# First transposes in four PSUM tiles, ones under the keys by fills, two sets of squares at other places, dense work rounded to the piece

## The chip, the cores and the metric

The kernel runs on one core of a Trainium2 chip. The metric is the device time in microseconds (us) of one execution; lower is better. The core has a matrix engine (TensorE; PE in the profile, PEld for its weight loads), VectorE (DVE), ScalarE (ACT), GpSimd (POOL) and SyncE (SP), which here only issues DMAs.

## The reference

The input `x` has 2048 rows of 512. It is normalised per row. From that come sliding-window attention with 32 heads of 16 and a window of 256 keys, and a gated feed-forward layer with 1792 hidden columns:

```python
xn = _layernorm(x)
# attention A: q, k, v = xn @ wqkv, per head
scores = q @ k.T * Dh ** -0.5          # key within 0..255 rows behind the query
s = (softmax(masked scores) @ v) @ wo
# feed-forward B
g = _silu((_silu(xn @ w1) * (xn @ w3)) @ w2)
return x + s * g
```

Input and output are float32.

## The kernel before

**Precision.** Each float32 operand of a dense product is split into two float16 halves, `hi` and `lo`, after scaling by a power of two. A dense product is three matmuls, hi x hi, hi x lo, lo x hi. To find the power of two of a weight, `squares` (L175 on ScalarE, L177 on VectorE) sums the squares of each row into `ssq`, a cast makes `sb` (L187), and `powers` (L200) sums `sb` over the partitions with a matmul against `onesb`; L202 to L211 turn that into the scale. The float16 halves are then made by `split` (L215 `hi` on ScalarE, L216 `lo` on VectorE) or by `split_pool` (L224, L225 on ScalarE, L221 on GpSimd).

**Tiles.** The rows are cut into four tiles of 512 (t = 0 to 3). `prepare(t)` loads four blocks of 128 rows, centres and scales them (L337), transposes each by four matmuls against the identity (L353) and makes `XH` (L356) and `XL` (L361). For t = 0 the transposes of two blocks write the two halves of one PSUM tile of the pool `pss`.

**Attention.** A group g is 8 heads. `project` makes q and k of a group (L421, evacuated by L430 and L434, stored to DRAM by L437 to L441), and `fetch` (L453) loads them back with three float16 terms of each head under one another, 48 rows, in partitions 0 to 47 and 64 to 111 of `KA[r]` (r = 0, 1, 2 in rotation) and of `qa`. Rows 48, 49, 112 and 113 of `KA` hold the constant 2^12 ("ones"), against which the same rows of `qa` carry the negative row maximum. A unit is (t, g, p), p being one half of a group's heads; there are 32. `pass1` makes scores (L474) and row maxima (L479) of the unit two ahead, `pass2` makes scores again (L521), adds masks (L530 over 1024 columns, L535 over 512), takes the exponential (L539) and multiplies by V (L549).

**Feed-forward.** The 1792 hidden columns are 14 blocks f. `load(0, f)` loads block f's float32 weights; `measure(f, 1)` squares those of blocks f and f + 1, finds their scales and makes float16 halves; `gate_up` multiplies (L682; L693 tanh, L697 product, L702, L706, L221 behind it), `down` accumulates (L727).

**Order.** On TensorE the instructions run in the order in which the kernel writes them. On the other engines the order was chosen when the program was built; `tc.issue_after(i)` puts what its block writes behind instruction i on i's engine. `later(n, f)` calls f at the n-th next `step()`; `step()` comes after each batch and each dense piece. `spread` puts the dense pieces of a unit (6 matmuls each, some 9 or 3) between its seven batches of scores; a batch is up to one `pass2` chunk and one or two `pass1` parts, and batches 2, 4 and 6 also run the products with V, counted as 6. `keep_busy(n)` runs n matmuls that nothing reads. PSUM has three buffers of the pool `psm` (tag "mm"), two of `pss` (two banks each) and one of `pso`.

The start, for orientation (before the change):

```python
keep_busy(22)
...
run([k00[0], q00[0], k00[1], q00[1]])
qk[1][2]()
qk[1][3]()
with tc.issue_after(lasts["hi"].ins):
    run([k00[2], q00[2]])
```

`qk[g]` are load, squares, scale and split of the q and k weights of group g; `wv` the same of the v weights.

Of the kernel before, what the change touches and what calls it, by code (L numbers as in the profile page):

```python
# [1 line left out]

# [6 lines left out]
F32 = mybir.dt.float32  # L9
BF16 = mybir.dt.bfloat16  # L10
F16 = mybir.dt.float16
I32 = mybir.dt.int32
AF = mybir.ActivationFunctionType
ALU = mybir.AluOpType
# [5 lines left out]
P = 128  # L20
# [9 lines left out]
TW = S // NT  # L30
KW = TW + 2 * P
WIN = 64 + 2 * P
FB = F // P
# [9 lines left out]
TERMS = 3  # L43
KR = TERMS * DH
ONE = 2.0**12
VW = DH + 1
VB = 10
SLOTS = 32
# [13 lines left out]
def tile_block(ctx: ExitStack, tc: tile.TileContext, x, wqkv, wo, w1, w3, w2, out):  # L62
    nc = tc.nc
# [18 lines left out]
    pss = pool("pss", 2, PSUM)  # L82
    pso = pool("pso", 1, PSUM)
# [5 lines left out]
    def take(dtype):  # L89
        slot = free.pop(0)  # L90
        made = fpool.tile([P, 512 if dtype == F32 else 1024], dtype, name=slot, tag=slot, bufs=1)
        held[id(made)] = slot, made
        return made

    def give(*tiles):
        for made in tiles:
            free.append(held.pop(id(made))[0])
# [14 lines left out]
    def later(n, f):  # L112
        made_so_far[0] += 1
        queue.append((now[0] + n, made_so_far[0], f))
# [93 lines left out]

    def scaled(a, by, name):
        t = const.tile([P, 1], F32, name=name)  # L210
        nc.vector.tensor_scalar(t, a, by, None, op0=ALU.mult)  # L211
        return t

    def split(hi, lo, raw, s):
# [91 lines left out]
    def prepare(t):  # L306

        mv = lnpool.tile([P, 4, 2], F32, name="mv")
        rs = lnpool.tile([P, 4], F32, name="rs")
        xts = {}  # L310
        pair = {}

        def load(b):
            xts[b] = take(F32)
            (nc.scalar if t == 0 and b % 2 else nc.sync).dma_start(xts[b], x[t * TW + b * P:t * TW + (b + 1) * P, :])

        def stats(b):
            st = lnpool.tile([P, nc.vector.BN_STATS_DIM], F32, name="st")
            nc.vector.bn_stats(st, xts[b])
            nc.vector.bn_aggr(mv[:, b, :], st)  # L320

        def rstd(b0, b1):
            ve = lnpool.tile([P, b1 - b0], F32, name="ve")
            nc.vector.tensor_scalar(ve, mv[:, b0:b1, 1], 1e-5, None, op0=ALU.add)

            r0 = lnpool.tile([P, b1 - b0], F32, name="r0")
            nc.vector.tensor_scalar(r0.bitcast(I32), ve.bitcast(I32), 1, None, op0=ALU.logical_shift_right)
            nc.vector.tensor_scalar(r0.bitcast(I32), r0.bitcast(I32), -1.0, float(0x5F3759DF), op0=ALU.mult, op1=ALU.add)
            sq = lnpool.tile([P, b1 - b0], F32, name="sq")
            for i in range(3):  # L330
                nc.vector.tensor_mul(sq, r0, r0)
                nc.vector.scalar_tensor_tensor(sq, sq, -0.5, ve, op0=ALU.mult, op1=ALU.mult)
                nc.vector.scalar_tensor_tensor(r0, sq, 1.5, r0, op0=ALU.add, op1=ALU.mult)
            nc.vector.tensor_scalar(rs[:, b0:b1], r0, XS, None, op0=ALU.mult)

        def centre(b):
            lasts["centre"] = nc.vector.tensor_scalar(xts[b], xts[b], mv[:, b, 0:1], rs[:, b:b + 1],  # L337
                                                      op0=ALU.subtract, op1=ALU.mult)

        def turn(b):  # L340
            if t not in X:
                X[t] = xpool.tile([P, NC, TW], F16, name="XH"), xpool.tile([P, NC, TW], F16, name="XL")
            xh, xl = X[t]
            c = slice(b * P, (b + 1) * P)
            if t:
                pt = psm.tile([P, NC, P], F32, name="mm", tag="mm")
            else:

                if b % 2 == 0:
                    pair["s"] = pss.tile([P, 2, 512], F32, name="s")  # L350
                pt = pair["s"][:, b % 2, :].rearrange("p (k q) -> p k q", q=P)
            for k in range(NC):
                nc.tensor.transpose(pt[:, k, :], xts[b][:, k * P:(k + 1) * P], identf)  # L353
            give(xts.pop(b))
            with urgent():
                lasts["xh"] = nc.scalar.copy(xh[:, :, c], pt)  # L356

            def rest():
                turned[t] = turned.get(t, 0) + 1
                with urgent():  # L360
                    lasts["x"] = nc.vector.tensor_sub(xl[:, :, c], pt, xh[:, :, c])  # L361
            later(1, rest)
        return load, stats, rstd, centre, turn
# [82 lines left out]
    def fetch(t, g):  # L446
        QA[t, g] = qa = qpool.tile([P, 4, TW], F16, name="qa")
        ka = keys(t, g)
        c0 = 0 if t else 2 * P
        for dst, d in ((ka[:, :, c0:], dK[g][:, :, t * TW - 2 * P + c0:(t + 1) * TW]),  # L450
                       (qa, dQ[g][:, :, t * TW:(t + 1) * TW])):
            for r in range(2):
                nc.sync.dma_start(dst[64 * r:64 * r + KR],  # L453
                                  d[64 * r:64 * r + 64].rearrange("(a d) i t -> (d i) a t", d=DH))
# [348 lines left out]
    def feed_forward():  # L803

        pieces = []
        late = []
        for t in range(NT):
            for f in range(FB):
                if t == 0:
                    if f % 2:  # L810
                        pieces += [(0, lambda f=f: load(0, f)) for f in range(f + 3, min(f + 5, FB))]
                    elif f + 2 < FB:
                        pieces.append((0, lambda f=f + 2: measure(f, 1)))
                    pieces += [(0, lambda k=k: measure_down(k)) for k, (_, f1) in enumerate(GROUPS) if f == f1 - 1]
                else:
                    if f == 0:
                        pieces += [(0, lambda t=t, f=f: load(t, f)) for f in range(2)]
                    if f + 2 < FB:
                        pieces.append((0, lambda t=t, f=f + 2: load(t, f)))
                if f == FB - 4 and t + 2 < NT:  # L820
                    first, second = prepare_beside(t + 2)
                    pieces += first
                pieces += [(6, q) for q in gate_up(t, f)]
                pieces += late
                late = []
                for k, (f0, f1) in enumerate(GROUPS):
                    if f == f1 - 1:
                        late = [q for b in range(4) for q in down(t, k, b)]
            if t + 2 < NT:
                pieces += second  # L830
        return pieces + late
# [48 lines left out]
    def spread(made, dense):  # L880

        whole = sum(c for c, _ in dense) + sum(c for c, _ in made)
        dense = list(dense)
        at = 0
        for k, (cost, batch) in enumerate(made):
            batch()
            step()
            at += cost
            while dense and (at < whole * (k + 1) / len(made) or dense[0][0] == 0):
                c, piece = dense.pop(0)  # L890
                at += c
                piece()
                if c:
                    step()
        run(dense)

    def run(dense):
        for c, piece in dense:
            piece()
            if c:  # L900
                step()
# [3 lines left out]
    qk = [weights_qk(g) for g in range(NG)]  # L905
    wv = weights("wv", wqkv[:, 2 * D:3 * D])
    wout = weights("wo", wo)
    ones = take(F16)
    nc.vector.memset(ones[0:4, 0:KW], ONE)
    for b in range(4):  # L910
        load0(b)
    qk[0][0]()
    qk[1][0]()
    wv[0]()
# [7 lines left out]
    for b in range(VB):  # L922
        nc.gpsimd.memset(V[:, b, 0:H * VW].rearrange("p (h w) -> p h w", w=VW)[:, :, DH:VW], 1.0)
    nc.gpsimd.memset(V[:, :, H * VW:], 0.0)


    def keep_busy(n):
        ps = psm.tile([P, 4, P], F32, name="ps", tag="mm")
        for _ in range(n):
            nc.tensor.matmul(ps, onesb, onesb.unsqueeze(1).to_broadcast([P, 4, P]), start=True, stop=True)  # L930

    keep_busy(22)
    for b in range(4):
        stats0(b)
    qk[0][1]()
    qk[0][2]()
    keep_busy(9)
    rstd0(0, 4)
    for b in range(4):
        centre0(b)  # L940
# [10 lines left out]
        flush()  # L951
    with tc.issue_after(lasts["hi"].ins), tc.issue_after(lasts["x"].ins):
        qk[1][1]()
        wv[1]()
    keep_busy(4)


    k00, q00 = (project(0, 0, k, ((0,), (1,), (2,))) for k in (1, 0))
    run([k00[0], q00[0], k00[1], q00[1]])
    qk[1][2]()  # L960
    qk[1][3]()
    with tc.issue_after(lasts["hi"].ins):
        run([k00[2], q00[2]])
# [10 lines left out]
        measure(0)  # L974
    run(project(0, 1, 0))
    later(1, lambda: fetch(0, 1))
    run(value(0))
    for r in range(3):
        for q in range(2):
            nc.sync.dma_start(KA[r][64 * q + KR:64 * q + KR + 2], ones[2 * q:2 * q + 2, 0:KW].unsqueeze(1).to_broadcast([2, 4, KW]))  # L980
    give(ones)
    qk[2][1]()
    run(value(1))
    qk[2][2]()
# [91 lines left out]
```

## Time and profile before

| | |
|---|---|
| median of 3 runs | 888.51 us (885.81 to 890.38) |
| profiled execution | 888.54 us |
| its span, first to last instruction | 886.8 us |
| mean granted TensorE clock | 0.994 |
| PE busy | 847.0 us (96%) |
| DVE, ACT, POOL busy | 623.7, 441.1, 193.4 us |

A row of the timeline has the start, the busy time, engine, line, operation, the names written and read, shapes, a count, and in square brackets the idle time of the engine before it with what ended it. PE can show overlapping matmuls, since matmuls are pipelined; consecutive matmuls of 512 columns start 0.215 us apart at the full clock.

### The profile page before, as it was taken

To read this page: it belongs to the slowest core of one execution; us is meant where nothing else is said; L and a number is where in the kernel's file an instruction comes from. 1 tells how busy PE (TensorE), PEld (TensorE's weight loads), DVE (VectorE), ACT (ScalarE), POOL (GpSimd) and SP (SyncE) were. 2 spreads that over 40 slices of the span, in tenths; PEclk is the share of its full clock that TensorE was granted. 3 is DMA by queue.
4 is the path that set the end of the run, shared out by engine and by line. 5 is a ranking of instruction groups with operands and counts; after the bars stand their busy time and mean duration, and the time that the engine had idled before them with its cause. 6 is when DMAs were issued, how large, how long until landed. Compare 5 with 4: busy or idle time off the path is not lost.

```text
span 886.8 us, 20443 instructions
## 1 busy us (share of the span) xinstructions
PE 847.0 (96%) x7814; PEld 375.9 (42%) x7814; DVE 623.7 (70%) x1833; ACT 441.1 (50%) x649; POOL 193.4 (22%) x308
## 2 busy tenths in 40 slices
PE   7968898999999999999999999999999999999997
PEld 3323344344444444444444444444444444444443
DVE  7676866797678667768767776777767786666435
ACT  4777767673435544443444444444444444444521
POOL 1236226352111202111111112120211103131211
PEclk9989999999999999999999999999999999999999
DMA  9864525646543343452445333533443353332201
GB/s 294 222 221 157 154 80 170 182 147 192 149 133 95 103 118 111 108 150 73 125 121 128 100 89 103 160 102 101 117 126 79 87 140 111 99 110 84 75 9 60
DMA packets 95133, 110.51 MB, mean 125 GB/s; under 512 B 16972, under 2 KB 60348, under 8 KB 95036
## 3 DMA queue, kind: packets, MB, share of 16 engines
q1 hardware_dynamic: 94748, 108.69, 42.9%
q8 instruction: 61, 1.00, 0.5%
q10 hardware_dynamic: 288, 0.52, 0.2%
q14 instruction: 36, 0.29, 0.1%
HBM read 76.28 MB, written 28.57 MB: 118 GB/s over the span
## 4 chain that ended last, share of the span: by engine, by line
PE 70%; DVE 9%; ACT 6%; DMA 5%; issue 5%; POOL 3%; SPq 1%; POOLq 0%; DVEq 0%; ACTq 0%
PE mm L682 25%; PE mm L727 14%; PE po L549 8%; PE mm L421 6%; PE s L521 6%; PE s L474 4%; PE mm L769 4%; PE mm L391 3%; DVE junk L479 3%; POOL slot L221 2%; DMA slot<-in_A_x_dram 1%; ACT pt L539 1%; DMA slot<-in_B_w_dram 1%; ACT sqa L175 1%; ACT slot L225 1%
## 5 line engine op out<-in xcount | busy, mean ns | idle before, releaser
L539 ACT ACTIVATE pt<-s,es 128x1024 f32<-128x1024 f32 (+1 forms) x184 | 200.9, 1094 | 224.0 <-DVE s L535 115.3
L682 PE MATMUL mm<-XH,slot 128*128 128x512 f16 x896 | 269.2, 382 | 1.6 <-DVE XL L361 1.2
L221 POOL TENSOR_TENSOR slot<-slot,slot 128x256 f16<-128x256 f32 (+1 forms) x220 | 146.9, 694 | 537.5 <-ACT slot L706 410.3
L479 DVE CUSTOM_DVE_ANT_0 junk<-s,MW 128x320 bf16<-128x320 f32 x448 | 218.0, 487 | 24.0 <-PE s L474 13.7
L682 PEld LDWEIGHTS <-slot 128*128 128x128 f16 x1344 | 121.7, 98 | 161.7 <-issue 29.4
L682 PE MATMUL mm<-XL,slot 128*128 128x512 f16 x448 | 170.5, 381 | 0.0
L727 PE MATMUL mm<-slot,slot 128*128 128x512 f16 x672 | 160.7, 383 | 1.7 <-DVE XL L361 1.4
L535 DVE TENSOR_TENSOR s<-s,M 128x512 f32<-128x512 f32 x128 | 89.0, 696 | 72.4 <-PE s L521 67.6
L549 PE MATMUL po<-pt,V 128*32 128x128 f32 (+1 forms) x1920 | 98.3, 330 | 0.0
L727 PEld LDWEIGHTS <-slot 128*128 128x128 f16 x672 | 61.1, 98 | 82.6 <-issue 16.3
L474 PE MATMUL s<-KA,qa 48*64 48x320 f16 (+2 forms) x1024 | 73.6, 298 | 12.6 <-DVE M L479 8.5
L530 DVE TENSOR_TENSOR s<-s,M 128x1024 f32<-128x1024 f32 x56 | 68.8, 1228 | 19.6 <-PE s L521 15.9
L521 PE MATMUL s<-qa,KA 50*64 50x128 f16 (+1 forms) x1920 | 74.2, 251 | 5.6 <-ACT pt L539 2.8
L521 PEld LDWEIGHTS <-KA 50*64 50x64 f16 x1920 | 33.7, 105 | 80.2 <-issue 47.4
L697 DVE SCALAR_TENSOR_TENSOR slot<-slot,mm 128x512 f32<-128x512 f32 x56 | 38.4, 685 | 41.3 <-ACT slot L693 41.1
L706 ACT CAST slot<-slot 128x512 f16<-128x512 f32 x56 | 34.5, 616 | 53.2 <-DVE slot L702 53.1
L549 PEld LDWEIGHTS po<-pt,V 128*32 128x32 f32 x1920 | 49.8, 109 | 24.8 <-issue 12.0
L693 ACT ACTIVATE slot<-mm,sgs 128x512 f32<-128x512 f32 x56 | 38.2, 682 | 27.5 <-PE mm L682 23.8
L702 DVE SCALAR_TENSOR_TENSOR slot<-mm,slot 128x512 f32<-128x512 f32 x56 | 38.6, 688 | 18.6 <-PE mm L682 18.5
L221 POOL TENSOR_TENSOR on<-on,rb 128x256 f32<-128x256 f32 x32 | 22.6, 727 | 127.9 <-DMA qa<-dm 82.9
L743 DVE SCALAR_TENSOR_TENSOR slot<-mm,dsc,slot 128x512 f32<-128x512 f32 x48 | 35.9, 749 | 20.5 <-PE mm L727 20.4
L421 PE MATMUL mm<-XH,whi 128*128 128x512 f16 x128 | 47.1, 381 | 1.2 <-ACT whi L215 1.2
(122 smaller groups left out, 828.1 us busy)
## 6 DMA issues: line engine op xcount, KB each, us to landing
slot<-dW SPq DMA_DIRECT2D x126, 256.0 KB
slot<-in_B_w_dram SPq DMA_DIRECT2D x42, 256.0 KB
dW<-slot SPq DMA_DIRECT2D x42, 256.0 KB
slot<-in_A_x_dram SPq DMA_DIRECT2D x30, 256.0 KB
KA<-dK SPq DMA_DIRECT2D x24, 288.0 KB
qa<-dQ SPq DMA_DIRECT2D x32, 192.0 KB
dK<-slot SPq DMA_DIRECT2D x16, 256.0 KB
dQ<-slot SPq DMA_DIRECT2D x16, 256.0 KB
```

The lines of the kernel that those rows point to most:

```text
L221: op(out[:, c], a[:, c], b[:, c])
L421: nc.tensor.matmul(cell["pp"], a[:, k, c, :], b[:, c, :], start=(c, i) == parts[0][0], stop=(c, i) == parts[-1][-1])
L474: nc.tensor.matmul(s[64 * c:64 * c + 64, r, :n], qa[rows, 2 * p + a, ii * P + 64 * c:ii * P + 64 * c + 64], ka[rows, 2 * p + a, e - n:e], ...
L479: nc.vector.tensor_tensor_reduce(out=junk[:, :n], in0=s[:, r, :n], in1=mask, scale=1.0, scalar=NEG, op0=ALU.add, op1=ALU.max, accum_out=M[ ...
L521: nc.tensor.matmul(s[h:h + 64, r, o:o + w * P], ka[rows, 2 * p + a, (j + 2) * P + h:(j + 2) * P + h + 64], qa[rows, 2 * p + a, q * P:(q + ...
L530: nc.vector.tensor_add(sv, sv, m.unsqueeze(1).to_broadcast([P, 4, 2, P]))
L535: nc.vector.tensor_add(sv[:, :, b, :], sv[:, :, b, :], M2[:, k:k + 1, :].to_broadcast([P, 4, P]))
L539: nc.scalar.activation(pt[:, :, 0:n], s.rearrange("p r (a q) -> p (r a) q", a=2)[:, :, 0:n], AF.Exp, scale=es)
L549: nc.tensor.matmul(cell["po"][32 * i:32 * i + 32, q * P:(q + w) * P], V[:, (4 * t + j) % VB, h * VW:h * VW + 32], pt[:, i, o:o + w * P], s ...
L682: nc.tensor.matmul(cell[k], w[:, (a * NC + c) * P:(a * NC + c + 1) * P], b[:, c, :], start=c == 0 and i == 0, stop=c == NC - 1 and i == 2)
L702: nc.vector.scalar_tensor_tensor(sg, cell[1], 0.5 * HS / (WS * XS)**2, sg, op0=ALU.mult, op1=ALU.mult)
L727: nc.tensor.matmul(ps, hh[:, a * TW + b * P:a * TW + (b + 1) * P], w[:, c * D:(c + 1) * D], start=f == f0 and i == 0, stop=f == f1 - 1 and ...
```

## The change

1. The first transposes (t = 0): each block has a PSUM tile of its own. Blocks 0 and 1 take a `pss` tile each, block 2 the `pso` tile, block 3 a `psm` tile.
2. The constant under the keys: six DMAs from a small tile `ones` (L980) go, and with it one of 32 slots is no longer held. In their place all of `KA[0]` is filled by VectorE, `KA[1]` by a ScalarE activation and `KA[2]` by four GpSimd fills, at the start. Rows that hold keys are overwritten by `fetch`.
3. Squares: those of `wv` come after the scale of `qk[1]` (on VectorE behind its last instruction), and `q00[1]` moves behind them; `measure(2)` is called before `value(0)` and no longer as a piece of the feed-forward list.
4. `spread` adds a dense piece when half of it still fits before the target (rounding), where it added pieces until the target was reached.
5. `keep_busy` counts 22, 9, 4 become 27, 5, 4.

```diff
+TWO_ONES = struct.unpack("f", struct.pack("ee", ONE, ONE))[0]
...
-        nc.vector.tensor_scalar(t, a, by, None, op0=ALU.mult)
+        lasts["scale"] = nc.vector.tensor_scalar(t, a, by, None, op0=ALU.mult)
...
-            if t:
+            if t or b == 3:
                 pt = psm.tile([P, NC, P], F32, name="mm", tag="mm")
+            elif b == 2:
+                pt = pso.tile([P, TW], F32, name="po").rearrange("p (k q) -> p k q", q=P)
             else:
-                if b % 2 == 0:
-                    pair["s"] = pss.tile([P, 2, 512], F32, name="s")
-                pt = pair["s"][:, b % 2, :].rearrange("p (k q) -> p k q", q=P)
+                pt = pss.tile([P, 2, 512], F32, name="s")[:, 0, :].rearrange("p (k q) -> p k q", q=P)
...
-                    elif f + 2 < FB:
+                    elif 0 < f < FB - 2:
                         pieces.append((0, lambda f=f + 2: measure(f, 1)))
...
-            while dense and (at < whole * (k + 1) / len(made) or dense[0][0] == 0):
+            while dense and (at + dense[0][0] / 2 <= whole * (k + 1) / len(made) or dense[0][0] == 0):
...
-    ones = take(F16)
-    nc.vector.memset(ones[0:4, 0:KW], ONE)
     for b in range(4):
         load0(b)
+    nc.vector.memset(KA[0].rearrange("p a c -> p (a c)").bitcast(F32), TWO_ONES)
+    nc.scalar.activation(KA[1].rearrange("p a (b c) -> p (a b) c", c=P), onesb.unsqueeze(1).to_broadcast([P, 24, P]),
+                         AF.Copy, scale=ONE)
...
+    for a in range(4):
+        nc.gpsimd.memset(KA[2][:, a, :].bitcast(F32), TWO_ONES)
...
-    keep_busy(22)
+    keep_busy(27)
...
-    keep_busy(9)
+    keep_busy(5)
...
         qk[1][1]()
+    keep_busy(4)
+    k00, q00 = (project(0, 0, k, ((0,), (1,), (2,))) for k in (1, 0))
+    run([k00[0], q00[0], k00[1]])
+    qk[1][2]()
+    with tc.issue_after(lasts["scale"].ins):
         wv[1]()
-    keep_busy(4)
-    k00, q00 = (project(0, 0, k, ((0,), (1,), (2,))) for k in (1, 0))
-    run([k00[0], q00[0], k00[1], q00[1]])
-    qk[1][2]()
+    run([q00[1]])
     qk[1][3]()
...
     later(1, lambda: fetch(0, 1))
+    measure(2, 1)
     run(value(0))
-    for r in range(3):
-        for q in range(2):
-            nc.sync.dma_start(KA[r][64 * q + KR:64 * q + KR + 2], ones[2 * q:2 * q + 2, 0:KW].unsqueeze(1).to_broadcast([2, 4, KW]))
-    give(ones)
```

More of the change, by code (lines that the diff above doesn't have):

```diff
@@ L1 @@
+import struct
 from contextlib import ExitStack, nullcontext
@@ L310, in prepare @@
         xts = {}
-        pair = {}
         def load(b):
@@ L953, in tile_block @@
         qk[1][1]()
-        wv[1]()
     keep_busy(4)
     k00, q00 = (project(0, 0, k, ((0,), (1,), (2,))) for k in (1, 0))
-    run([k00[0], q00[0], k00[1], q00[1]])
+    run([k00[0], q00[0], k00[1]])
     qk[1][2]()
+    with tc.issue_after(lasts["scale"].ins):
+        wv[1]()
+    run([q00[1]])
     qk[1][3]()
```

## The prediction

> **What bounds the kernel now.** The page of the profile comes first.
>
> ```profile
> span 886.8 us, 20443 instructions
> ...
> PE 847.0 (96%) x7814; PEld 375.9 (42%) x7814; DVE 623.7 (70%) x1833; ACT 441.1 (50%) x649; POOL 193.4 (22%) x308
> ...
> PEclk9989999999999999999999999999999999999999
> ```
>
> TensorE is busy for 96% of the span, so an edit is worth the idle time of TensorE that it removes or adds, and the time at the lower clock. The third slice and the waits of TensorE say where that lies; the last three numbers are total us, times, longest us.
>
> ```profile
> PE s L474 <- DVE M L479: 8.5, 10, 2.0
> PE ps L200 <- DVE sb L187: 7.4, 3, 5.3
> ...
> PE s L353 <- ACT XH L356: 1.4, 2, 0.7
> PE mm L421 <- ACT whi L215: 1.2, 1, 1.2
> ```
>
> One wait of 5.3 us stands at L200, the matmul that sums squares. The table of stretches shows its place and its price (columns: length, busy us of PE, PEld, DVE, ACT, POOL with counts, clock, DMA share, GB/s).
>
> ```profile
> 35.00:40.00 5.00, 5.00 (x31) 2.12 (x29) 2.54 (x14) 5.00 (x10) 4.59 (x7) 1.00 0.77 156
> ...
> 45.00:50.00 5.00, 2.13 (x10) 0.88 (x9) 3.03 (x9) 2.37 (x7) 1.41 (x2) 0.92 1.11 360
> 50.00:55.00 5.00, 2.55 (x14) 0.87 (x14) 2.70 (x16) 4.12 (x15) 0.22 (x1) 0.50 0.47 130
> ```
>
> After the wait the clock is 0.50. ScalarE, on the other hand, has nothing free between 30 and 40 us. The timeline of the first 53 us names the links:
>
> ```profile
> 14.37 0.66 PE L353 MATMUL s<-identf,slot 128*128 128x128 f32 x4 [0.73 <-ACT XH L356]
> ...
> 18.17 0.16 DVE L187 CAST sb<-ssq 128x2 bf16<-128x2 f32 x1
> ...
> 20.14 0.15 DVE L202 TENSOR_SCALAR al<-ps 128x1 f32<-128x1 f32 x1
> ...
> 31.73 0.38 PE L391 MATMUL mm<-wvh,XH 128*128 128x512 f16 x1 [0.26 <-DVE al L202]
> ...
> 52.22 0.17 DVE L187 CAST sb<-ssq 128x6 bf16<-128x6 f32 x1 [1.97 <-ACT sqa L175]
> 52.45 0.17 PE L200 MATMUL ps<-sb,onesb 128*128 128x6 bf16 x1 [5.32 <-DVE sb L187]
> ```
>
> Last, the later units, where TensorE is nearly never idle: two batches of scores that need a mask over 1024 columns (L530), one with 18 dense matmuls behind it, one with 12.
>
> ```profile
> 288.52 0.42 PE L521 MATMUL s<-qa,KA 50*64 50x128 f16 x16
> ...
> 289.35 0.69 DVE L697 SCALAR_TENSOR_TENSOR slot<-slot,mm 128x512 f32<-128x512 f32 x1 [1.64 <-ACT slot L693]
> ...
> 291.27 1.11 ACT L539 ACTIVATE pt<-s,es 128x1024 f32<-128x1024 f32 x1 [1.96 <-DVE s L530]
> ...
> 293.00 0.41 PE L521 MATMUL s<-qa,KA 50*64 50x256 f16 x8
> ```
>
> ```profile
> 337.06 0.42 PE L521 MATMUL s<-qa,KA 50*64 50x128 f16 x16
> ...
> 338.86 1.11 ACT L539 ACTIVATE pt<-s,es 128x1024 f32<-128x1024 f32 x1 [1.85 <-DVE s L530]
> ...
> 340.24 0.41 PE L521 MATMUL s<-qa,KA 50*64 50x256 f16 x8
> ```
>
> The next scores reuse the PSUM tile that the exponential reads. With 18 matmuls they come 4.48 us after the first scores, with 12 after 3.18 us (so six cost 1.30). The exponential ends 2.91 us after the first score (339.97) when nothing is in its way, and after 3.86 us (292.38) when the product L697 stands ahead of the mask on VectorE.
>
> **Step 1, first transposes.** Blocks 0 and 1 share one tile and 2 and 3 another, so a block's transposes wait for the copy of the block before: 0.68 and 0.73 us in the timeline. With four tiles they follow the centred blocks (L337 ends at 10.5, 11.05, 11.5, 12.0) and ScalarE copies without a break: the weight's copy (11.14 to 11.86), then four copies at a pitch of 0.56 end at 14.1 instead of 15.64. Gain 1.5. The block in the "mm" pool holds one of three buffers until L361 has read it. The row at 31.73 shows that a buffer is handed out as soon as any is free (it waits for `al`, the reader of the newest one, while L434 still reads an older), so the next projection takes the buffer of the warm-up matmuls; were it to wait, it would stand until about 16.9 and the gain would be 0. The tile of block 2 is next wanted at 85.8 (L549): free. The warm-up matmuls go from 22, 9, 4 to 27, 5, 4; they fill time before 9.28 and before the transposes, and the 5 end at 10.4, before the first centred block. Nothing.
>
> **Step 2, `qk[1][2]` ahead of the squares of `wv`.** Between `sb` (18.33) and `al` (20.14) VectorE does three squares of 0.69 while TensorE has the sum at 19.37; TensorE then waits 1.24 for the scaled weights at 22.35. With the squares queued behind the scale, that wait goes: 1.0, since the copies of `whi` (0.72) still follow. Queued behind are the two squares on VectorE (1.4), and what waits for them is the sum for `wv` at 24.4, with 4.3 to spare. At worst nothing is gained, at best 1.4.
>
> **Step 3, `measure(2)` early.** Its four squares on ScalarE run at 49.65 to 52.2, behind those of `qk[3]` (48.41), whose weights are asked for at 38.38. Issued before `value(0)` they need only weights asked for by 18.6. The wait of 5.32 at L200 goes, and with it the half clock: eight matmuls at a pitch of 0.43 for 0.215, and two smaller gaps, 1.9 in all. Against it, ScalarE is full from 25.6 to 41.2, and the squares (4 x 0.61 = 2.45) now stand before those of `qk[2]` (32.0 to 33.2). Their sum is due at 34.3 on TensorE; it would have its operand at 33.4 + 2.45 + 0.2 = 36.1, a new wait of 1.9 (all these times move earlier alike with steps 1 and 2). Behind it wait the first batch of `pass1` and `value(2)`. From below the cost is 0 (ScalarE takes `qk[2]` first), from above 5.3 and the half clock again; I take 1.9, since two waits of 1.7 and 1.9 us (at 74.3 and 64.8) left the clock at 1.00, while 2.2 us at 101.5 halved it. [...]
>
> **Step 4, ones by fills.** Off SyncE's queue go six issues (0.84, 0.67, 0.64, 0.63, 0.62, 0.62: 4.0 us), four of them right ahead of the loads of `qk[3]` and of blocks 4 and 5. SyncE is no bound then. VectorE: 768 elements took 0.70, so 1536 words take 1.0 to 2.8, from 1.55 and inside its idle time up to 4.45. ScalarE: 512 elements take 0.72, so 3072 take 2.6 to 4.3, from 2.95; its first square starts at 6.77, so at worst 0.5 late, and `sb` at 9.07 has that much from VectorE's own queue. GpSimd: four fills of some 0.6, from 3.95, with its next work at 35.1. The loads into the three tiles wait for the fills and come 20 us later. I take 0 (bounds -1 and +0.5).
>
> **Step 5, rounding.** Worked through by hand for a unit of 78 dense matmuls and three value groups counted as 6 each (96 over seven batches, 13.7 each), the old rule puts 18, 12, 6, 18, 6, 12, 6 behind the batches, the new one 12, 18, 6, 12, 6, 18, 6. From unit 8 on, batches 0 and 3 hold the two 1024-column masks. So 33 of the 44 places behind a heavy mask shrink from 18 to 12, one from 15 to 9, four grow. What precedes batches 0 and 3 stays the same, so the chains measured there should stay. With 3.18 us a free chain (2.91) still fits and a blocked one (3.86) costs 0.68. Summing each chain's overrun over units 8 to 28 in the timeline gives 3.0 behind batch 0 and 3.3 behind batch 3. The seven places that have 12 behind a 1024-column mask now lose 0.46, 0.68 and five times nothing: 0.16 each, 5.3 for 33. Before batch 6 there are 18 instead of 12; the waits there (0.89 and 0.70) may halve, -0.8. I take 6.3 - 0.8 = +5.5; bounds 0 (VectorE's order changes) and 15 (below). In units 0 to 7 heavy masks sit in batch 1 and gain cover, others lose it: 0.
>
> **Sum.** Against the profiled execution of 888.54 (span 886.8, 1.7 outside it, and 0.03 from the median of 888.51): -1.5 - 1.0 - 5.3 - 1.9 + 1.9 + 5.5 = -2.3, so **886.2**.
>
> **Rivals.** (A) *The tighter places cost nothing*, because masks get ahead of L697: 888.54 - 7.8 = 880.7. For it: a free chain leaves 0.27. Against it: the order on VectorE is that of the program here, and eleven of 44 chains overrun. 0.25. (B) *The wait moves instead of shrinking*: ScalarE does the scaling of blocks 0 and 1 (2.4 each) before the squares of `measure(2)`, and L200 stands 5.5 us some 15 us earlier, clock and all. Then 3.6 + 1.9 come back: 891.7. For it: ScalarE's ten full microseconds. Against: the squares are older in the program than that scaling. 0.18. (C) *Slower: the product stands ahead of the mask at two of three tight places*, 33 x 2/3 x 0.68 = 15 for the 5.5: 895.7. It decides once the tight places lose over 12.2 us, 0.37 each. For: VectorE is 70% busy, and chains of up to 4.32 occur. Against: a quarter are so now. 0.16. If the shared tile is not what makes the transposes wait, the forecast loses its 1.5 and stays inside its own band (883 to 890).
>
> **How the numbers follow.** The forecast has 0.41. A change of 0.5% (884.1 and 893.0) is about what can be told from none, the three runs lying 0.5% apart. Of the forecast 0.11 lies below 884.1 and 0.01 above 893.0; A is faster; B is within with 0.12 and slower with 0.06; C is slower. That makes 0.36, 0.41, 0.23. The range 878 to 895.5 leaves out a tenth on either side: below it A with waits at 64.8 and 101.5 gone too, above it most of C.
>
> **What would show it.** Four transposes without idle time and L356 ending near 14; `al` of `qk[1]` right behind its sum; no wait over 2 us at L200 and a clock of 1.00 from 45 to 60; no L980; scores behind heavy masks after 3.18 us where the chain is free and 3.9 where L697 is ahead. I am wrong if L200 waits over 3 us earlier on, or if TensorE's idle time between 280 and 840 falls or grows by over 10.

## The result and the profile after

Nine runs of each kernel, taken by turns, gave a median of 886.12 us before and 883.03 us after: a ratio of 0.9962 (95% interval 0.9947 to 0.9977), 3.1 to 3.4 us less. The forecast was 2.3 us less (886.2 on 888.54, a ratio of 0.9974); the range held. The profiled executions lie further apart, 888.54 and 881.5 us, since the one of before is 2.4 above its kernel's median and the one of after 1.5 below, the lowest of its nine; sizes below are therefore taken from ratios, and the traces are read mainly for places.

The page of the profile after, in the rows shown for before:

```profile
span 879.6 us, 20432 instructions
...
PE 846.5 (96%) x7815; PEld 376.5 (43%) x7815; DVE 626.7 (71%) x1833; ACT 443.1 (50%) x650; POOL 193.9 (22%) x312
```

TensorE is busy for as long as before (846.5 against 847.0); what went is idle time. Its waits (total us, times, longest):

```profile
PE s L523 <- ACT pt L541: 6.6, 8, 1.6
PE s L476 <- DVE M L481: 5.2, 8, 1.1
...
PE ps L203 <- DVE sb L190: 2.9, 3, 1.6
```

Line numbers are two or three higher than before. The wait of 5.3 at the sum of squares (L200, now L203) is gone, its longest is 1.6. At the head of the list now stands the wait of the scores (L523, before L521) for the exponential, 6.6 us in all. The stretches where the long wait was, in the columns used before:

```profile
45.00:50.00 5.00, 4.57 (x31) 1.74 (x28) 4.19 (x12) 5.00 (x15) 4.84 (x8) 1.00 1.04 353
50.00:55.00 5.00, 4.45 (x32) 1.98 (x32) 3.41 (x23) 5.00 (x12) 0.60 (x1) 1.00 0.59 184
```

TensorE is busy for 9.0 of these 10 us instead of 4.7, and the clock stays at 1.00. The timeline of the start has the forecast links:

```profile
11.58 0.66 PE L355 MATMUL po<-identf,slot 128*128 128x128 f32 x4
12.19 0.63 PE L355 MATMUL mm<-identf,slot 128*128 128x128 f32 x4
...
13.43 0.59 ACT L358 CAST XH<-mm 128x512 f16<-128x512 f32 x1
...
16.75 0.19 PE L203 MATMUL ps<-sb,onesb 128*128 128x1 bf16 x2
...
16.98 0.16 DVE L205 TENSOR_SCALAR al<-ps 128x1 f32<-128x1 f32 x1 [0.28 <-PE ps L203]
...
34.01 0.19 PE L203 MATMUL ps<-sb,onesb 128*128 128x1 bf16 x2 [1.55 <-DVE sb L190]
```

The blocks' transposes follow one another and the last copy of `XH` ends at 14.02 (14.1 was forecast, 15.64 it was; the weight's copy comes third among the five and not first). `al` of `qk[1]` comes right behind its sum. At 34.0 is the new wait for the squares of `qk[2]`: 1.55 (1.9 forecast).

Last, the scores of unit 8 behind which the second 1024-column mask stands; before, these were the rows at 288.52 to 293.00, with 18 dense matmuls behind the scores, now there are 12:

```profile
279.72 0.42 PE L523 MATMUL s<-qa,KA 50*64 50x128 f16 x16
...
280.55 0.69 DVE L699 SCALAR_TENSOR_TENSOR slot<-slot,mm 128x512 f32<-128x512 f32 x1 [1.64 <-ACT slot L695]
...
282.47 1.11 ACT L541 ACTIVATE pt<-s,es 128x1024 f32<-128x1024 f32 x1 [1.96 <-DVE s L532]
...
283.23 0.08 DVE L481 DVE_READ_ACCUMULATOR2_ANT M<- 128x1 f32 x1
...
283.36 0.41 PE L523 MATMUL s<-qa,KA 50*64 50x256 f16 x8 [0.39 <-DVE M L481]
...
283.64 0.33 PE L476 MATMUL s<-KA,qa 48*64 48x320 f16 x4
```

The product L699 again stands ahead of the mask, and the exponential starts 2.75 us after the first score in both kernels and ends 3.86 us after it. The next scores come after 3.64, where a free chain lets them come after 3.18. The bracket names what they waited for: not the exponential, which still runs until 283.58, but the row maxima L481 of `pass1`, which end at 283.31. So they took the other of the two `pss` tiles, and the tile of the exponential went to the next `pass1` scores, which start at 283.64. The forecast had the next scores wait for the exponential's tile (they do where the chain is free: those at 340.24 before wait for ScalarE); a chain with the product ahead costs 0.46 us here (and 0.46 behind batch 0 of unit 14, 416.76 to 420.40), not 0.68.

TensorE is 7.2 us ahead of the trace of before at unit 0 (66.94 against 74.18), 8.8 at unit 8 (269.16 against 277.96) and 7.2 at unit 31 (823.9 against 831.1).

### The profile page after: what moved, and what is told of

Its sections match the earlier page's. It is cut to its first block, busy times and chain, and to the rows that moved or that the text cites. A ratio compares the mean times of both kernels' runs of the same rounds, so it can differ in the third digit from the quotient of the medians.

```text
span 879.6 us, 20432 instructions
## 1 busy us (share of the span) xinstructions
PE 846.5 (96%) x7815; PEld 376.5 (43%) x7815; DVE 626.7 (71%) x1833; ACT 443.1 (50%) x650; POOL 193.9 (22%) x312
## 4 chain that ended last, share of the span: by engine, by line
PE 70%; DVE 11%; ACT 5%; issue 4%; DMA 4%; POOL 3%; SPq 2%; POOLq 0%; DVEq 0%; ACTq 0%
PE mm L684 24%; PE mm L729 13%; PE po L551 8%; PE mm L423 6%; PE s L523 6%; PE mm L771 4%; PE s L476 4%; PE mm L393 3%; DVE junk L481 3%; POOL slot L224 2%; DVE s L532 2%; ACT pt L541 1%; DMA slot<-in_A_x_dram 1%; DMA slot<-in_B_w_dram 1%; SPq L590 1%
## 5 line engine op out<-in xcount | busy, mean ns | idle before, releaser
L481 DVE CUSTOM_DVE_ANT_0 junk<-s,MW 128x320 bf16<-128x320 f32 x448 | 218.0, 487 | 27.3 <-PE s L476 16.2
L523 PE MATMUL s<-qa,KA 50*64 50x128 f16 (+1 forms) x1920 | 74.2, 251 | 9.9 <-ACT pt L541 6.6
L523 PEld LDWEIGHTS <-KA 50*64 50x64 f16 x1920 | 34.0, 105 | 85.1 <-issue 48.2
L699 DVE SCALAR_TENSOR_TENSOR slot<-slot,mm 128x512 f32<-128x512 f32 x56 | 38.3, 684 | 35.2 <-ACT slot L695 35.1
L745 DVE SCALAR_TENSOR_TENSOR slot<-mm,dsc,slot 128x512 f32<-128x512 f32 x48 | 35.9, 748 | 19.6 <-PE mm L729 19.4
```

Source lines behind the costliest of these rows:

```text
L481: nc.vector.tensor_tensor_reduce(out=junk[:, :n], in0=s[:, r, :n], in1=mask, scale=1.0, scalar=NEG, op0=ALU.add, op1=ALU.max, accum_out=M[ ...
L523: nc.tensor.matmul(s[h:h + 64, r, o:o + w * P], ka[rows, 2 * p + a, (j + 2) * P + h:(j + 2) * P + h + 64], qa[rows, 2 * p + a, q * P:(q + ...
```

## The experiments

Each was timed in five rounds against the kernel before on the same chip (three sets, each on a chip of its own); ratios are to before, with 95% intervals, and versions of different sets are compared by them. Theory T is the sum of the prediction.

**The rule of `spread`, taken out of the changed kernel and put into the one before.**

```diff
# e1_after_old_rule
-while dense and (at + dense[0][0] / 2 <= whole * (k + 1) / len(made) or dense[0][0] == 0):
+while dense and (at < whole * (k + 1) / len(made) or dense[0][0] == 0):
# e2_before_rounding: the same lines the other way round, in the kernel before
```

> The changed kernel with the old rule of spread (pieces added until the target is reached); all else as changed. Theory T (the prediction's sum: the start gains 7.8 us, rounding costs 5.5): 886.1 - 7.8 = 878.3, that is 4.7 below the changed kernel's 883.0, and first scores behind a 1024-column mask come 4.48 us later where 18 matmuls stand behind. Rival A (rounding is free, the start gains only the 3.1 that was measured): 883.0, no difference from the changed kernel.

> The kernel before with the new rule of spread alone. T: 886.1 + 5.5 = 891.6. A: 886.1. If the difference here and that of the changed kernel with the old rule disagree by over 2 us, the two parts act on one another.

The changed kernel with the old rule took 878.35 us, ratio 0.9916 (0.9901 to 0.9932); the kernel before with the new rule 889.98, ratio 1.0052 (1.0033 to 1.0071). So rounding costs (0.9962 - 0.9916) x 885.5 = 4.1 us in the one and 4.6 in the other. T holds (5.5 forecast), A falls, and within the noise the two parts do not act on one another. The waits of TensorE, first of the changed kernel with the old rule, then of the kernel before with the new:

```profile
PE s L523 <- ACT pt L541: 2.4, 4, 0.8
```

```profile
PE ps L200 <- DVE sb L187: 7.0, 3, 5.3
PE s L521 <- ACT pt L539: 6.6, 8, 1.6
```

The wait of the scores for the exponential is 2.4 us with the old rule (2.8 in the kernel before) and 6.6 with the new, in either kernel; the scores' wait for the row maxima grows with it (2.2 to 2.9 and 2.5 to 3.2). The wait of 5.3 stays where the start is the old one.

**Is it the masks?** The new rule was kept and the chunks of a unit put in another order, so that both 1024-column masks have 18 matmuls behind them.

```diff
# e6_wide_masks_at_1_5
-CHUNKS = (((-2, 0, 1), (3, 3, 1)), ((-1, 0, 2),), ((0, 0, 2),), ((0, 2, 1), (1, 3, 1)), ((1, 1, 2),), ((2, 2, 2),))
+CHUNKS = (((-1, 0, 2),), ((-2, 0, 1), (3, 3, 1)), ((0, 0, 2),), ((1, 1, 2),), ((2, 2, 2),), ((0, 2, 1), (1, 3, 1)))
```

> The changed kernel, new rule, with the chunks of a unit in another order: the two with a mask over 1024 columns in batches 1 and 5 instead of 0 and 3, so that both have 18 dense matmuls behind them under the new rule. Theory T (rounding costs what the chains behind these masks overrun): the cost goes, 3 to 5 below the changed kernel's ratio of 0.9962 to before (about 0.992). Rival E (the cost of rounding lies in the order of the dense pieces themselves): no change, ratio 0.996.

876.89 us, ratio 0.9903 (0.9885 to 0.9921): 5.2 us below the changed kernel. The list of waits does not show why; its row for the exponential is nearly as long as in the changed kernel:

```profile
PE s L523 <- ACT pt L541: 5.8, 8, 1.6
```

The gaps from first score to first score do. The table has the time from the first scores of unit 8 to those of unit 30, and what the gaps behind the 1024-column masks have beyond the shortest that the same number of dense matmuls leaves there (3.18 us with 12, 3.83 with 15, 4.48 with 18; the few places with other numbers are left out; in the new order the second gap also holds batch 6).

| one execution of | units 8 to 29 | behind the masks (chains) |
|---|---|---|
| before | 532.1 us | 4.9 us (11) |
| before, new rule | 533.1 us | 7.8 us (16) |
| changed | 533.7 us | 8.4 us (16) |
| changed, old rule | 531.0 us | 4.9 us (10) |
| changed, new order of chunks | 528.9 us | 1.4 us (2) |

Rounding makes the chains behind the wide masks overrun by some 3 us more, and 18 matmuls behind both masks take nearly all of it away, so the cover is what rounding costs; E falls. The new order gives more than rounding took, since with the old rule too 10 or 11 chains overrun. That order under the old rule was not run.

**The early `measure(2)`, taken out and put in.**

```diff
# e3_after_measure_late
-                    elif 0 < f < FB - 2:
+                    elif f + 2 < FB:
...
-    measure(2, 1)
# e4_before_measure_early: the same lines the other way round, in the kernel before
```

> The changed kernel with measure(2) back at its place in the feed-forward list. T: the wait of 5.3 us at the sum for measure(2), and the half clock behind it (1.9), come back and the new wait of 1.7 us at the sum for qk[2] goes: 883.0 + 5.5 = 888.5. Rival D (the wait came from the weights of qk[3], which are now asked for earlier since the six DMAs of ones are gone): the wait shrinks to under 3 us and the time is within 2 of 883.

> The kernel before with measure(2) called before value(0), nothing else changed. T: the wait of 5.3 us and the half clock go, a wait of 1.9 us at the sum for qk[2] comes: 886.1 - 5.3 = 880.8. Rival D: the gain needs the room on SyncE's queue and is under 2 us.

In the kernel before the early squares gain what was forecast: 879.74 us, ratio 0.9940 (0.9921 to 0.9959), 5.3 us; D, which had under 2 there, is wrong on this one. The wait of 5.32 is gone and one of 1.55 stands at the sum for `qk[2]`, but in this trace the sum for `qk[3]`, whose loads still go out at 38.6, now waits 2.17 (at 56.39). In the changed kernel taking the early squares out does not lose 5.5, it gains 2.7 by the ratios: 879.96 us, 0.9932 (0.9917 to 0.9948) against 0.9962. T fails here. D had the wait right and the time (within 2 us of 883) not quite. The timeline of the changed kernel with the late squares has the sum for `measure(2)` with a wait of 0.86 in place of 5.32:

```profile
46.07 0.17 PE L203 MATMUL ps<-sb,onesb 128*128 128x6 bf16 x1 [0.86 <-DVE sb L190]
```

The new wait of 1.55 at the sum for `qk[2]` is gone here. By unit 0 this trace is 1.0 us ahead of the changed kernel's; where the rest of the 2.7 comes from is not shown.

**The fills alone.** The kernel before with step 4 and nothing else.

```diff
# e5_before_fills
-    ones = take(F16)
-    nc.vector.memset(ones[0:4, 0:KW], ONE)
...
+    nc.vector.memset(KA[0].rearrange("p a c -> p (a c)").bitcast(F32), TWO_ONES)
...
-    for r in range(3):
-        for q in range(2):
-            nc.sync.dma_start(KA[r][64 * q + KR:64 * q + KR + 2], ones[2 * q:2 * q + 2, 0:KW].unsqueeze(1).to_broadcast([2, 4, KW]))
-    give(ones)
```

> The kernel before with the ones by fills instead of the six DMAs, nothing else changed. The prediction gave this step 0 (bounds -1 and +0.5). Rival D (the wait of 5.3 us for the squares of measure(2) is a wait for the weights of qk[3], whose loads stand behind four of those DMAs on SyncE's queue): the loads of qk[3] are issued before 36 us instead of at 38.4, the wait falls under 2 us, the clock stays at 1.00 from 50 to 55 us, and the time is 4 to 7 below before.

877.74 us, ratio 0.9909 (0.9891 to 0.9927): 8.1 us by the ratio, a little over D's 4 to 7. The prediction gave this step 0. SyncE's queue shows why; first the kernel before, then this one:

```profile
35.64 2.64 SPq L980 DMA_DIRECT2D KA<-slot  x4
38.38 0.95 SPq L271 DMA_DIRECT2D slot<-in_A_wqkv_dram  x2
```

```profile
19.43 0.99 SPq L273 DMA_DIRECT2D slot<-in_A_wqkv_dram  x2
```

The loads of `qk[3]` are issued at 19.4 instead of 38.4. (Between the first of the six DMAs, at 19.53, and the last four, SyncE of the kernel before issues stores and fetches of the first projections and waits for them, once 3.9 us; the loads stand behind all of this.) Its squares, and those of `measure(2)` behind them on ScalarE, begin at 39.87 instead of 48.41. The sum for `measure(2)` comes at 47.80 without a wait, though nothing was moved for that; this is all that is left of waits at such sums:

```profile
PE ps L202 <- DVE sb L189: 1.2, 2, 0.6
```

The clock is 1.00 from start to end of the work in this execution. In the changed kernel, which also has the other steps, the two loads go out at 30.7 and 34.7, earlier than before but not as early as with the fills alone.

**The place on the queue or the DMAs themselves?** All six DMAs kept, written after the loads of `qk[3]`.

```diff
# e11_before_ones_later
     run(value(0))
-    for r in range(3):
...
-    give(ones)
     qk[2][1]()
...
     qk[3][0]()
+    for r in range(3):
...
+    give(ones)
```

> The kernel before, its six DMAs of ones kept, only written after the loads of qk[3] instead of ahead of them. Theory D (what the fills brought is the place of those loads on SyncE's queue): the loads of qk[3] are issued before 30 us, the wait of 5.3 us for the squares of measure(2) falls under 2 us and the time is 4 to 8 below before (ratio 0.991 to 0.995). Rival (the DMAs themselves, their 4 us on the queue or the slot that they hold, cost the time): less than 2 us, ratio above 0.998.

880.46 us, ratio 0.9940 (0.9922 to 0.9958), 5.3 us less. The loads are issued at 19.6, and this is all that is left of waits at the sum of squares, the longest of them at the first sum, 9 us into the span:

```profile
PE ps L200 <- DVE sb L187: 2.7, 2, 2.1
```

So D holds for most of what the fills bring: it is the place of those loads. The 2.7 us between this ratio and that of the fills are not attributed: the cost of the DMAs themselves can be in them. Other transfers stand in another order too, and in this execution, the slowest of its six, the clock was 0.81 from 45 to 50 us and 0.85 from 50 to 55.

**Steps 1 and 2 taken out of the changed kernel, one at a time.**

```diff
# e8_after_shared_tiles
+        pair = {}
...
-            if t or b == 3:
+            if t:
                 pt = psm.tile([P, NC, P], F32, name="mm", tag="mm")
-            elif b == 2:
-                pt = pso.tile([P, TW], F32, name="po").rearrange("p (k q) -> p k q", q=P)
             else:
-                pt = pss.tile([P, 2, 512], F32, name="s")[:, 0, :].rearrange("p (k q) -> p k q", q=P)
+                if b % 2 == 0:
+                    pair["s"] = pss.tile([P, 2, 512], F32, name="s")
+                pt = pair["s"][:, b % 2, :].rearrange("p (k q) -> p k q", q=P)
# e10_wv_squares_early
         qk[1][1]()
+        wv[1]()
...
-    run([k00[0], q00[0], k00[1]])
+    run([k00[0], q00[0], k00[1], q00[1]])
     qk[1][2]()
-    with tc.issue_after(lasts["scale"].ins):
-        wv[1]()
-    run([q00[1]])
```

> The changed kernel with the first transposes in two shared tiles as before. T: 1.5 us slower than the changed kernel (ratio 0.998 against 0.9962), the first projection starting near 15.5 instead of 14.1 us. Rival: the start waits elsewhere and nothing changes.

> The changed kernel with the squares of wv and q00[1] where they were before (step 2 undone). T: 1.0 us slower than the changed kernel, ratio 0.9973 against 0.9962, with three squares of VectorE between the sum and the scale of qk[1] again. Rival: TensorE waits for something else there and nothing changes.

With shared tiles 883.4 us, ratio 0.9974 (0.9962 to 0.9987), 1.1 us slower than the changed kernel; the waits for the copies are back, and the first projection starts at 15.39 instead of 14.07:

```profile
PE s L356 <- ACT XH L359: 1.5, 2, 0.9
```

With the early squares of `wv` 882.91 us, ratio 0.9968 (0.9955 to 0.9980), 0.5 us slower. TensorE's wait for the scaled weights of `qk[1]` is back with 1.1 us, but the intervals overlap so widely that the size of either step is not settled, only the place.

**Versions that beat both.**

```diff
# e7_old_rule_measure_late: the changed kernel with the edits of e1 and e3
# e9_wide_1_5_measure_late: the changed kernel with the edits of e6 and e3
```

> The changed kernel with the old rule and with measure(2) at its old place. If the two effects found (4.1 from the rule, 2.1 from leaving measure(2) where it was) add: ratio to before 0.9916 + 0.9932 - 0.9962 = 0.9886, some 10 us below before. If the wait that the early squares make is covered under the old rule: 0.9916, as with the old rule alone.

> The changed kernel, new rule, with the chunks with a mask over 1024 columns in batches 1 and 5 and with measure(2) back at its old place. If the two gains found on the changed kernel (5.2 us for the chunks' order, 2.1 for measure(2)) add: ratio to before 0.9903 - 0.0030 = 0.987, some 11 us below before and level with or below the kernel with the old rule and late measure (0.9883). If the places behind the masks and the late start share one slack, 0.990.

The first took 875.73 us, ratio 0.9883 (0.9862 to 0.9905), as the sum of the two gains had it (0.9886); the second 876.09 us, 0.9886 (0.9870 to 0.9901), where the sum had 0.987 and shared slack 0.990, so it doesn't tell these apart. The first has the lowest median of all, some 7 us below the changed kernel (the second lies within its interval); it keeps the fills, the four tiles and the late squares of `wv`, and drops the rounding and the early `measure(2)`.

## Why the prediction was right

The sign and the size came out (-2.3 forecast, -3.1 to -3.4 measured). The waits of steps 1, 2 and 3 went or came where they were forecast, and the cost of rounding lies at the place named. But steps 3 and 4 were right only as a pair, and part of the closeness is luck: steps 1 and 2 gave some 0.9 less than forecast, step 5 cost some 1.4 less, and these misses work against each other.

- **Step 1** (1.5): 1.1 by the ratios; the copies ended within 0.1 us of the time forecast.
- **Step 2** (1.0): 0.5, not settled; the wait of 1.24 it named returned as 1.1 when it was undone.
- **Step 3** (5.3 and 1.9, less a new 1.9): true of the kernel before, where it gained 5.3 alone. The new wait stood where it was forecast, with 1.55. In the changed kernel the step is a loss: leaving it out gains 2.7, 2.9 under the old rule and 1.5 with the new order of chunks, since step 4 had taken most of the old wait away already (0.86 is left of it) and the new one was the price.
- **Step 4** (0, bounds -1 and +0.5): this is the step that failed. Alone it is worth 8.1 (most of it, 5.3, for the place of the loads on the queue). The text had the links: the squares of `measure(2)` stand behind those of `qk[3]`, whose loads stand behind four of the DMAs. It then said that SyncE is no bound, and so ended the chain at ScalarE's order instead of following it on to the queue. The total did not suffer because steps 3 and 4 remove the same wait, which was counted once: 8.1 less 2.7 is 5.4 for the pair, and 5.3 was forecast. The costs of the fills were as bounded or less: 1.34 us on VectorE, 2.76 on ScalarE, 1.49 on GpSimd, all in idle time.
- **Step 5** (+5.5): 4.1 and 4.6. The place held, with too high a price and one wrong link. In the traces the chains behind the masks lose 3.5 us more than before (8.4 against 4.9), where 6.3 was forecast, and the gaps over batch 6 lose 0.9 less (0.8 forecast). The forecast took a chain with the product ahead at 0.68, by the end of the exponential; four of the 16 that overrun cost 0.46, where the next scores got the tile of the row maxima instead, and the dearest costs 1.74 (unit 11). By the table, rounding takes 2.7 us in one execution of the changed kernel, while the ratios have 4.1; the profiled execution is the fastest of its nine, and where the others lose the rest is not known.
- **Rivals.** A (the tighter places are free) and C (they lose over 12) fall by the first two experiments, B (the early squares only move the wait) by the 1.55.

As sums: the fills 8.1, four tiles 1.1, squares of `wv` 0.5, less 2.7 for the early squares and 4.1 for the rounding, leave 2.9; 3.1 to 3.4 was measured. The fills were put into the kernel before and the others taken out of the changed one, and each has an interval of 1 to 2 us on either side, so this agreement is a check and no proof.

## What to carry to other kernels

When a wait goes back through an engine's order to a transfer, follow it on to the queue that issues the transfer and look at what stands ahead there: four of six small DMAs, 2.64 us of issuing, stood right ahead of two loads that went out 19 us earlier without them. Two edits that cure one wait are worth it once, and the dearer one may then be a loss, so take each out of the whole before keeping both. When dense work is spread between batches, give it to the batches whose chains are longest rather than evenly.

## What the runs showed of the hardware

In these traces the granted clock does not follow the length of a wait alone. By the brackets of the rows, TensorE idled for 2.04 us up to 103.75 in the kernel before (the prediction's 2.2 at 101.5; its 1.7 and 1.9 read 1.53 and 1.72, with the clock at 1.00 behind both) and for 2.18 us up to 89.36 after, and both times the granted clock then was 0.50 for 3.41 us (103.86 to 107.27 before, 90.01 to 93.42 after). At the wait of 5.32 before, up to 52.45, it was 0.50 for 6.83 us (49.24 to 56.07). The rows after:

```profile
85.00:90.00 5.00, 2.60 (x30) 1.02 (x22) 3.69 (x13) 1.85 (x4) 1.24 (x2) 1.00 0.27 77
90.00:95.00 5.00, 5.00 (x19) 1.91 (x20) 4.17 (x23) 4.31 (x8) 2.61 (x5) 0.66 0.25 66
```

The kernel before with the fills also has a wait of 2.18 us (up to 95.55), and the mean granted clock of that execution is 1.000. What tells this wait from the 2.18 us after is not shown. Behind the new wait of step 3, 1.55 us up to 34.01 after, the clock stayed at 1.00 (1.00 from 30 to 40 us).
